# u's spectrum blocks loaded by 128 partitions, and inverse transforms moved between the product loop and the waits behind it

## The chip, the core and the metric

The kernel runs on one core of one Trainium2 chip. The metric is the device time of one execution, in microseconds (us). All arithmetic that matters here is float32 or float32r on TensorE (PE), with VectorE (DVE), ScalarE (ACT) and GpSimd (POOL) around it; SyncE (SP), ScalarE and GpSimd issue the transfers.

## What is computed

The reference takes a sequence u of 2048 steps by 512 channels, and runs two blocks on it, each behind a layer norm with learned shift, scale and gate (`sa, ca, ga, sb, cb, gb`, from `silu(c) @ w_mod`):

```
h = layernorm(u) * (1 + ca) + sa
K[d, l] = Re sum_n C[d, n] * exp(dt[d] * A[d, n] * l) * dt[d] * B[d, n]      l = 0 .. 2047
y = irfft(rfft(h, 4096) * rfft(K, 4096))[:2048] + h * Dskip                  per channel
x = u + ga * y
h = layernorm(x) * (1 + cb) + sb
z = gelu(layernorm(h) @ w1), its four channel quarters shifted by +1, -1, +2, -2 steps
x1 = h + z @ w2
out = x + gb * (x1 + gelu(layernorm(x1) @ w3) @ w4)
```

## The kernel before

The kernel is one hand-ordered program; the order in which its Python functions are called is the order of instructions on every engine. It has four parts.

**Part 1** (`turns`, `products`, `burst`, up to about 213 us) builds the convolution kernel K in `KX`, norms u, and takes the first half of the Fourier transform of u (`u_dft`). Its results go to a DRAM buffer `VU` of [2 channel halves, 64 rows, 64 columns, 256 channels]. The 64 rows are real and imaginary parts of 32 frequencies; which row holds what follows from the columns of the constant `FU`. VU's rows are real parts of frequencies 0 to 31, then the imaginary ones.

**Part 2** is a loop over 16 steps `(jh, kc)`: two channel halves `jh`, eight groups `kc` of four frequencies. Step n does `spectrum_k(n)` (the second half of K's transform, line 667), `multiply(n)` on VectorE (lines 678 to 683), `back(n-1)` (the first half of the inverse transform, line 693; ScalarE evicts `z`, and GpSimd writes it to the DRAM buffer `ZT[jh]`) and `spectrum_u(n+1)` (line 644), which needs u's block. `load_vu` (line 633) brings a block in by two transfers on SP, one for the real parts to partitions 0 to 63 and one for the imaginary parts to partitions 64 to 127, three steps ahead. The last step's two writes of `z` are issued by ScalarE.

Inside the loop's later turns the second half of the inverse transform for the first channel half runs: `load_inv(0, g)` reads two blocks of `ZT[0]`, and `inverse(0, g)` is two calls of `inv_half` (line 722), each of four matmuls into a PSUM tile, and an addition on VectorE (line 725) into `X2`, the residual. There are four groups g of four sequence blocks. Groups 0 to 2 are transformed in turns 11 to 13, group 3 behind the loop. `ldw1` and `ldw2` load w1 and w2 in two parts each; the `split` they return makes a high and a low part on ScalarE and VectorE (line 744).

All of these loads take their buffers in turn from one pool of seven (`ldp`, tile name `ld`), so a load waits for the readers of the buffer seven places earlier.

**The waits.** `ZT[1]` can only be read when its last write has landed. Behind the loop stand `inverse(0, 3)`, ten statistics of first halves (`half_stat`), and filler matmuls, `keep(n)` (line 1140), n products of w1 with itself into a tile that nobody reads. Then come the transforms of the second channel half in the order in which the mixer needs them: group 3's second part (blocks 14 and 15, mixer group 7), then `a00`, `a30`, `a01` (group 0's first part, group 3's first, group 0's second), and `a10`, `a11` (group 1). A name like `a00` stands for the addition of that part on VectorE; its matmuls are issued where `inv_half` is called. SP issues the loads in this order, group 1 and group 2 as whole blocks of 512 KB, the others as 256 KB. A second `keep` stands behind `a01`'s matmuls.

**Part 3 and 4**, the token mixer (`mix_mod1`, `mix_mod2`, `mix_norm`, `transposed`, `parts_of`, `mix_half`, lines 762 to 828) and the channel mixer (`chan`, lines 860 to 961), follow by groups of two blocks. For one mixer group: VectorE modulates and takes statistics (`mix_mod2`, lines 765 and 758), GpSimd makes the reciprocal deviation (lines 753, 754, 814, 815), ScalarE norms, TensorE transposes (line 790), ScalarE and VectorE split the transposes (`nh`, `nl`, line 798), and TensorE does 24 products for each of two halves (lines 825 to 828).

Of the kernel before, what the change touches and what calls it, by code (L numbers as in the profile page):

```python
# [12 lines left out]
PSUM = bass.MemoryType.PSUM  # L13
# [14 lines left out]
def shape_constants():  # L28
    f = lambda x: np.ascontiguousarray(x.astype(np.float32))
    k1, k2, q = np.arange(32), np.arange(64), np.arange(32)  # L30
    c2b = lambda c: np.where(c < 32, 31 - c, c)
    th = 2 * np.pi * (k1[None] + .5) * q[:, None] / 64
    W = np.stack([np.cos(th), -np.sin(th)], 1)
    FU = np.zeros((4, 32, 2, 2, 2, 32))
    for h in range(2):
        for cp2 in range(2):
            cp = 2 * h + cp2
            FU[1 - cp if cp < 2 else cp, :, h, cp2] = W
    FK = np.zeros((2, 2, 32, 2, 64))
    FK[:, 0, :, 0] = FK[:, 1, :, 1] = W.reshape(32, 64)  # L40
    b = c2b(np.arange(64))
    al = 2 * np.pi * b[:, None, None] * ((k1[None, :, None] + .5) / 4096 + k2[None, None, :] / 64)
    c, s = np.cos(al), np.sin(al)
    T2 = np.stack([np.stack([c, -s], 2), np.stack([s, c], 2)]).reshape(128, 32 * 128)
    T3 = np.stack([s, -s]).reshape(128, 32 * 64)
    h, cq, cp2 = np.meshgrid(np.arange(2), np.arange(16), np.arange(2), indexing='ij')
    b = c2b((2 * h + cp2) * 16 + cq).reshape(64)
    al = 2 * np.pi * b[None, :] * k2[:, None] / 64
    c, s = np.cos(al), np.sin(al)
    Gm = np.zeros((64, 2, 64, 2))  # L50
    Gm[:, 0, :, 0], Gm[:, 0, :, 1], Gm[:, 1, :, 0], Gm[:, 1, :, 1] = c, s, -s, c
    Gm = np.tile(Gm.reshape(64, 256), (2, 1))
    FI = np.zeros((2, 2, 32, 16, 2, 2, 32))
    for hh in range(2):
        for c2 in range(2):
            for cc in range(16):
                bb = int(c2b(np.array((2 * hh + c2) * 16 + cc)))
                th = 2 * np.pi * (k1[:, None] + .5) * (bb + 64 * q[None]) / 4096
                FI[c2, 0, :, cc, hh, bb // 16 - 2 * hh] = np.cos(th) * (2 / 4096)
                FI[c2, 1, :, cc, hh, bb // 16 - 2 * hh] = -np.sin(th) * (2 / 4096)  # L60
    eye = np.eye(16)
    j = np.arange(32)
    c0 = np.tile((eye[:, :, None] * (j + .5)).reshape(16, 512), (2, 1))
    C0 = np.zeros((2, 2, 32, 2, 512))
    C0[:, 0, :, 0], C0[:, 1, :, 1] = c0, c0
    C0 = C0.reshape(128, 1024)
    e1 = (eye[:, :, None] * j).reshape(16, 512)
    e2 = (eye[:, :, None] * np.ones(32)).reshape(16, 512)
    C1 = np.concatenate([e1, e1, e2, e2] * 2, 0)
    ex0 = np.concatenate([np.arange(31, -1, -1), np.arange(32, 64)])  # L70
    ex1 = np.concatenate([64 * np.arange(8), 512 * np.arange(4)])
    CE = np.concatenate([(eye[:, :, None] * ex0.reshape(2, 32)[:, None, None, :]).transpose(1, 0, 2, 3).reshape(16, -1),
                         np.zeros((16, 64 * NX1))], 1)
    CE = np.tile(CE, (8, 1))
    for u in range(4):
        CE[u * 32:u * 32 + 32, 1024 + u * 16 * NX1:1024 + (u + 1) * 16 * NX1] = \
            np.tile((eye[:, :, None] * ex1).reshape(16, -1), (2, 1))
    PA = np.zeros((2, 4, 16, 2, 2, 4, 2, 16))
    PB = np.zeros((4, 2, 16, 4, 4, 2, 4, 16))
    for e in range(16):  # L80
        for v in range(2):
            for u in range(4):
                for p in range(2):
                    PA[v, u, e, v, p, u, p, e] = 1
        for c in range(8):
            for p in range(4):
                PB[c // 2, c % 2, e, c // 4 * 2 + c % 2, p, 1 - c // 2 % 2, p, e] = 1
    return {k: f(v) for k, v in dict(
        FU=FU.reshape(128, 256), FK=FK.reshape(128, 128), T2=T2, T3=T3, G=Gm,
        FI=FI.reshape(128, 16 * 128), C0=C0, C1=C1, CE=CE, PA=PA.reshape(128, 512), PB=PB.reshape(128, 2048), ID=np.eye(128)).items()}  # L90
# [16 lines left out]
def dram(t, off, ap):  # L107
    return bass.AP(tensor=t.tensor, offset=t.offset + off, ap=ap)


def body(ctx, tc, A):
    nc = tc.nc
    V, S, P, T, Y = nc.vector, nc.scalar, nc.gpsimd, nc.tensor, nc.sync
# [74 lines left out]
    FU = ph.tile([128, 2, 128], F32, name="FU")  # L188
# [440 lines left out]

    def load_vu(jh, kc):  # L630
        t = vus[jh, kc] = block()
        for ri in range(2):
            Y.dma_start(t[ri * 64:ri * 64 + 64],
                        dram(VU, jh * 1048576 + (ri * 32 + kc * 4) * 16384, [[256, 64], [16384, 4], [1, 256]]))

    def spectrum_u(jh, kc):
        vu = vus.pop((jh, kc))
# [48 lines left out]
    def back(jh, kc):  # L686
        zc = zcs.pop((jh, kc))
        z = s2.tile([128, 4, 256], F32, name="z")
        o = [psa.tile([128, 2, 256], F32, name="pz") for kk in range(2)]
        for n in range(2):  # L690
            for kk in range(2):
                r = slice(kk * 64, kk * 64 + 64)
                T.matmul(o[kk], Gm[r, n], zc[n][r], start=(n == 0), stop=(n == 1))  # L693
        for kk in range(2):
            act(z[:, 2 * kk:2 * kk + 2], o[kk])
            if (jh, kc) == (1, 7):
                S.dma_start(ZT[jh][:, kc * 4 + 2 * kk:kc * 4 + 2 * kk + 2], z[:, 2 * kk:2 * kk + 2])
        if (jh, kc) != (1, 7):
            P.dma_start(ZT[jh][:, kc * 4:kc * 4 + 4], z)

    def load_inv(jh, g, i=None, qs=(Y, Y)):
        if (jh, g) not in zis:
            zis[jh, g] = [block() for h in range(2)]
        for h in range(2):
            c0 = 12 - 4 * g if h == 0 else 4 * g
            a, n = (0, 4) if i is None else (2 * (i if h else 1 - i), 2)
            qs[h].dma_start(zis[jh, g][h][:, a:a + n],  # L707
                            dram(ZT[jh], (h * 16 + c0 + a) * 32768, [[256, 128], [32768, n], [1, 256]]))
# [18 lines left out]
    def inverse(jh, g):  # L727
        for i in range(2):
            inv_half(jh, g, i, psy, "py")()
# [353 lines left out]
    with tc.manual_schedule():  # L1083
# [12 lines left out]
        for n, st in enumerate(steps):  # L1096
            p = spectrum_k(*st)
            multiply(*st, us, p)
            if n == 7:
                v0x.close()  # L1100
                pw2 = ctx.enter_context(pool("pw2", side="right", reuse_waits="tile"))
                pw1 = ctx.enter_context(pool("pw1", side="right", reuse_waits="tile"))
                W2h, W2l, ldw2 = weights(pw2, A["w2"], 512, 512, "w2", 4)
                W1h, W1l, ldw1 = weights(pw1, A["w1"], 512, 512, "w1", 4)
            if n > 0:
                back(*steps[n - 1])
            if n < 15:
                us = spectrum_u(*steps[n + 1])
            if n + 3 < 16:
                load_vu(*steps[n + 3])  # L1110
            if n == 0:
                load_t2(1)
            if n == 1:
                Y.dma_start(T3[:, 16:], t3[:, 16:])
            if n in (3, 4, 6, 8):
                load_x(n - 3 if n < 5 else n // 2 - 1)
            if n == 9:
                Y.dma_start(FI, A["FI"].rearrange("p (a b c) -> p a b c", a=16, b=2))
            if split:
                split()  # L1120
                split = None
            if n in (8, 9, 14, 15):
                split = (ldw1 if n < 10 else ldw2)(two, n % 2 * 2, 2)
            if 9 <= n < 13:
                load_inv(0, n - 9)
            if 11 <= n < 14:
                inverse(0, n - 11)
        back(*steps[15])
        split()
        s2x.close()  # L1130
        tp = lambda name, bufs=1, **k: pool(name, bufs, reuse_waits="tile", **k)
        cm = ctx.enter_context(tp("cm", 2, side="right"))
        hv = ctx.enter_context(tp("hv", side="right"))
        gop = ctx.enter_context(tp("gop", 2, side="right"))
# [8 lines left out]
        load_inv(1, 0, 0, (Y, S))  # L1143
        load_inv(1, 3, 0)
        load_inv(1, 0, 1)
        inverse(0, 3)
        for b in (14, 15, 0, 1, 2, 3, 4, 5, 6, 7):
            half_stat(b, 0)
        load_inv(1, 1)
        keep(14)  # L1150
        inv_half(1, 3, 1, psy, "py")()
        first_stats(7)
        load_inv(1, 2)
        a00 = inv_half(1, 0, 0, psy, "py")
        a30 = inv_half(1, 3, 0, psw, "pm")
        a01 = inv_half(1, 0, 1, psw, "pm")
        keep(22)
        mix_mod1(7)
        a00()
        mix_mod2(7, 0)  # L1160
        mix_mod2(7, 1)
        mix_norm(7)
        first_stats(0)
        a30()
# [2 lines left out]
        hl = parts_of(transposed(mh.pop(7)[0]))  # L1167
        mix_mod2(0, 0)
        mix_mod2(0, 1)
        a10 = inv_half(1, 1, 0, psy, "py")  # L1170
        a11 = inv_half(1, 1, 1, psy, "py")
        mix_half(7, hl, 0)
        mix_norm(0)
        first_stats(1)
# [95 lines left out]
```

## Time and profile before

| | us |
|---|---|
| three runs | 718.76, 717.22, 712.0 |
| median | 717.22 |
| profiled execution | 716.82 |
| its span, first to last instruction | 715.1 |
| TensorE busy | 671.7 |
| VectorE busy | 506.3 |
| ScalarE busy | 335.6 |
| mean granted TensorE clock | 0.993 |

Instructions stand in the profile by engine, line and operation, with the tile written and the tiles read. Matmuls are PE and weight loads PEld. ScalarE's instructions all have line 119, that of a helper. "issue" as what ended an idle time says that the engine waited for nothing that the profile shows. SPq, ACTq and POOLq are the transfers that these engines issue. The granted clock is a share of full speed.

### The profile page before, as it was taken

How to read it: one execution, taken by the hardware profiler on the slowest of the kernel's cores; microseconds unless marked ns; L12 is line 12 of the kernel's file. 1: busy time of each engine (PE TensorE's matmuls, PEld its weight loads, DVE VectorE, ACT ScalarE, POOL GpSimd, SP SyncE). 2: the span in 40 equal slices, each digit the busy share in tenths (PEclk: the TensorE clock that was granted, in tenths of full speed). 3: DMA queues.
4: the chain of work that ended last, by engine and by line, in shares of the span. 5: the costliest groups of instructions: out<-in, count | busy, mean ns of one | idle time of the engine just before them, and what ended most of it. 6: DMA issues, size and time to landing. Idle time of an engine off the chain costs nothing.

```text
span 715.1 us, 16869 instructions
## 1 busy us (share of the span) xinstructions
PE 671.7 (94%) x7083; PEld 520.1 (73%) x7083; DVE 506.3 (71%) x847; ACT 335.6 (47%) x549; POOL 85.6 (12%) x191
## 2 busy tenths in 40 slices
PE   2689999999999899998899999999999999999997
PEld 1356655666568566664688889989898998989896
DVE  8989999999986566767978868557463635454422
ACT  2768898889956255634245623313123121212121
POOL 1011212112000001100463200201010000000000
PEclk9999999999999999999999999999999999999999
DMA  8452274744439999793649402011020111111011
GB/s 286 152 129 69 74 217 102 191 128 116 132 80 266 232 289 315 224 324 144 217 149 302 132 5 56 15 45 31 16 74 16 49 27 31 31 30 30 0 30 31
DMA packets 56884, 85.52 MB, mean 120 GB/s; under 512 B 5764, under 2 KB 43656, under 8 KB 55144
## 3 DMA queue, kind: packets, MB, share of 16 engines
q1 hardware_dynamic: 52648, 66.61, 34.8%
q0 software_dynamic: 3136, 16.52, 6.4%
q10 hardware_dynamic: 1024, 1.31, 0.6%
q8 instruction: 56, 0.92, 0.5%
q14 instruction: 20, 0.16, 0.1%
HBM read 58.20 MB, written 31.85 MB: 126 GB/s over the span
## 4 chain that ended last, share of the span: by engine, by line
PE 48%; DVE 2%; ACT 1%; DMA 1%; SPq 0%; issue 0%; POOL 0%; DVEq 0%; ACTq 0%
PE pm L825 7%; PE pm L828 7%; PE pm L826 7%; PE pa L949 6%; PE pa L941 6%; PE pa L942 5%; PE ph L879 2%; PE ph L880 2%; PE ph L882 2%; PE pT L790 2%; DMA ld<-ZT 1%; PE pT L1140 1%; PE py L722 1%; ACT nh L119 0%; DVE st L758 0%; SPq L707 0%
## 5 line engine op out<-in xcount | busy, mean ns | idle before, releaser
L119 ACT ACTIVATE gh<-pm 128x512 fp32r<-128x512 f32 (+1 forms) x48 | 26.9, 560 | 200.7 <-PE pm L828 200.7
L825 PE MATMUL pm<-nh,w3h 128*128 128x256 f32 (+1 forms) x352 | 85.8, 279 | 0.9 <-ACT nh L119 0.9
L826 PE MATMUL pm<-nh,w3l 128*128 128x256 f32 (+1 forms) x352 | 85.6, 279 | 0.1
L933 DVE TENSOR_TENSOR gl<-gf,gh 128x512 fp32r<-128x512 f32 (+1 forms) x48 | 30.8, 642 | 68.4 <-ACT gf L119 68.4
L941 PE MATMUL pa<-w4h,gh 128*128 128x512 f32 (+1 forms) x176 | 69.6, 396 | 0.0
L942 PE MATMUL pa<-w4l,gh 128*128 128x512 f32 (+1 forms) x176 | 68.9, 392 | 0.0
L825 PEld LDWEIGHTS pm<-nh,w3h 128*128 128x128 f32 (+1 forms) x352 | 65.3, 185 | 2.6 <-ACT nh L119 1.1
L826 PEld LDWEIGHTS pm<-nh,w3l 128*128 128x128 f32 (+1 forms) x352 | 65.2, 185 | 2.2 <-DVE w3l L744 0.5
L828 PE MATMUL pm<-nl,w3h 128*128 128x256 f32 (+1 forms) x352 | 54.8, 277 | 0.0
L949 PE MATMUL pa<-w4h,gl 128*128 128x512 f32 (+1 forms) x176 | 48.1, 391 | 0.8 <-DVE gl L933 0.8
L458 PE MATMUL xx<-MG,ON 64*128 64x512 f32 x160 | 48.0, 396 | 0.0
L457 PE MATMUL xx<-MG,ON 64*128 64x512 f32 x160 | 48.0, 396 | 0.0
L828 PEld LDWEIGHTS pm<-nl,w3h 128*128 128x128 f32 (+1 forms) x352 | 46.7, 185 | 0.2 <-DVE nl L798 0.2
L753 POOL TENSOR_TENSOR rs<-mv,eps_t 128x1 f32<-128x1 f32 (+1 forms) x39 | 11.4, 293 | 279.0 <-DVE mv L759 266.6
L678 DVE TENSOR_TENSOR ma<-pk,us 128x512 f32<-128x512 f32 x32 | 21.9, 685 | 30.7 <-issue 22.9
L119 ACT ACTIVATE z<-pz 128x512 f32<-128x512 f32 x32 | 17.5, 595 | 54.6 <-PE pz L693 38.3
L885 DVE TENSOR_TENSOR h<-h,ph 128x512 f32<-128x512 f32 x16 | 11.0, 686 | 45.2 <-PE ph L882 45.2
L475 DVE SCALAR_TENSOR_TENSOR e<-tr,p 128x512 f32<-128x512 f32 x64 | 41.0, 682 | 2.1 <-ACT tr L119 1.9
L949 PEld LDWEIGHTS pa<-w4h,gl 128*128 128x128 f32 (+1 forms) x176 | 33.0, 188 | 8.3 <-DVE gl L933 1.2
L484 DVE TENSOR_TENSOR e<-tr,p 128x1024 f32<-128x1024 f32 x32 | 38.9, 1217 | 0.0
L507 PEld LDWEIGHTS kp<-e,e 128*32 128x32 f32 x2048 | 30.0, 110 | 12.2 <-issue 8.1
L485 DVE TENSOR_TENSOR e<-tr,m 128x1024 f32<-128x1024 f32 x32 | 38.9, 1216 | 0.0
(234 smaller groups left out, 1763.5 us busy)
## 6 DMA issues: line engine op xcount, KB each, us to landing
VU<-vs SPq DMA_DIRECT2D x64, 128.0 KB, 3.5
ld<-VU SPq DMA_DIRECT2D x32, 256.0 KB, 10.4
ZT<-z POOLq DMA_DIRECT2D x15, 512.0 KB, 8.3
ld<-ZT SPq DMA_DIRECT2D x12, 512.0 KB, 8.2
Dw<-in_w POOLq DMA_DIRECT2D x8, 688.0 KB, 4.7
xu<-in_u SPq DMA_DIRECT2D x16, 256.0 KB, 6.8
KX<-in_u SPq DMA_DIRECT2D x16, 256.0 KB, 10.2
GD<-go SPq DMA_DIRECT2D x16, 256.0 KB, 2.3
```

What stands on the lines that cost most here:

```text
L119: return S.activation(out, in_, f, bias=bias, scale=scale)
L457: T.matmul(x[:, :512], la, ma, start=(i == 0), stop=(i == len(ops) - 1))
L458: T.matmul(x[:, 512:], lb, mb, start=(i == 0), stop=(i == len(ops) - 1))
L475: V.scalar_tensor_tensor(e0[:, 1, a], tr[:, 1, 0], 1.0 - 2.0 * a, mg[:, a], op0=OP.mult, op1=OP.mult)
L484: V.tensor_mul(e0[:, 0], tr[:, 0, 0:1].to_broadcast([128, 2, 512]), mg)
L485: V.tensor_mul(e1.rearrange("p r d q -> p r (d q)"), tr[:, :, 1], m1s[0][:, u % 2:u % 2 + 1].to_broadcast([128, 2, 512]))
L825: T.matmul(p, wh[:, k, c], hi[k], start=(k == 0), stop=False)
L826: T.matmul(p, wl[:, k, c], hi[k], start=False, stop=False)
L828: T.matmul(p, wh[:, k, c], lo[k], start=False, stop=(k == 3))
L941: T.matmul(acc[i], gh[:m, e, s], W4h[:m, f], start=(f == 0), stop=False)
L942: T.matmul(acc[i], gh[:m, e, s], W4l[:m, f], start=False, stop=False)
L949: T.matmul(acc[i], gl[:m, e, s], W4h[:m, f], start=False, stop=(f == 10))
```

## The change

Five things change.

- The columns of `FU` are reordered, so that VU's row 2k is the real and row 2k+1 the imaginary part of frequency k. A block of u then is one access pattern over 128 partitions, and `load_vu` issues one transfer of 512 KB.
- Of the last step's two writes of `z`, SP issues the first and ScalarE the second.
- `inverse(0, 0)` and `inverse(0, 1)` are in turns 11 and 13, `inverse(0, 2)` moves behind the loop, ahead of `inverse(0, 3)`; `load_inv(0, 3)` moves from turn 12 to 13.
- The second part of w2 is loaded behind group 1's blocks of the second half, and split behind `mix_mod2(0, 1)`.
- The matmuls of `a10` and `a11` move from behind the transposes of mixer group 7 to ahead of the second `keep`, with a PSUM pool `psz` of their own; the two `keep` shrink from 14 to 7 and from 22 to 15; and `a00` moves behind `mix_mod2(7, 1)`.

```diff
--- before.py
+++ after.py
@@ -36,6 +36,7 @@
         for cp2 in range(2):
             cp = 2 * h + cp2
             FU[1 - cp if cp < 2 else cp, :, h, cp2] = W
+    FU = FU.reshape(128, 2, 2, 2, 32).transpose(0, 1, 2, 4, 3)
     FK = np.zeros((2, 2, 32, 2, 64))
     FK[:, 0, :, 0] = FK[:, 1, :, 1] = W.reshape(32, 64)
     b = c2b(np.arange(64))
@@ -629,9 +630,7 @@
 
     def load_vu(jh, kc):
         t = vus[jh, kc] = block()
-        for ri in range(2):
-            Y.dma_start(t[ri * 64:ri * 64 + 64],
-                        dram(VU, jh * 1048576 + (ri * 32 + kc * 4) * 16384, [[256, 64], [16384, 4], [1, 256]]))
+        Y.dma_start(t, dram(VU, jh * 1048576 + kc * 8 * 16384, [[256, 128], [32768, 4], [1, 256]]))
 
     def spectrum_u(jh, kc):
         vu = vus.pop((jh, kc))
@@ -694,7 +693,7 @@
         for kk in range(2):
             act(z[:, 2 * kk:2 * kk + 2], o[kk])
             if (jh, kc) == (1, 7):
-                S.dma_start(ZT[jh][:, kc * 4 + 2 * kk:kc * 4 + 2 * kk + 2], z[:, 2 * kk:2 * kk + 2])
+                (Y, S)[kk].dma_start(ZT[jh][:, kc * 4 + 2 * kk:kc * 4 + 2 * kk + 2], z[:, 2 * kk:2 * kk + 2])
         if (jh, kc) != (1, 7):
             P.dma_start(ZT[jh][:, kc * 4:kc * 4 + 4], z)
 
@@ -1119,16 +1118,16 @@
             if split:
                 split()
                 split = None
-            if n in (8, 9, 14, 15):
+            if n in (8, 9, 14):
                 split = (ldw1 if n < 10 else ldw2)(two, n % 2 * 2, 2)
-            if 9 <= n < 13:
-                load_inv(0, n - 9)
-            if 11 <= n < 14:
-                inverse(0, n - 11)
+            if n in (9, 10, 11, 13):
+                load_inv(0, n - 9 if n < 12 else 3)
+            if n in (11, 13):
+                inverse(0, n // 2 - 5)
         back(*steps[15])
-        split()
         s2x.close()
         tp = lambda name, bufs=1, **k: pool(name, bufs, reuse_waits="tile", **k)
+        psz = a2.enter_context(tp("psz", 2, space=PSUM, side="right"))
         cm = ctx.enter_context(tp("cm", 2, side="right"))
         hv = ctx.enter_context(tp("hv", side="right"))
         gop = ctx.enter_context(tp("gop", 2, side="right"))
@@ -1143,22 +1142,26 @@
         load_inv(1, 0, 0, (Y, S))
         load_inv(1, 3, 0)
         load_inv(1, 0, 1)
+        inverse(0, 2)
         inverse(0, 3)
         for b in (14, 15, 0, 1, 2, 3, 4, 5, 6, 7):
             half_stat(b, 0)
         load_inv(1, 1)
-        keep(14)
+        split = ldw2(two, 2, 2)
+        keep(7)
         inv_half(1, 3, 1, psy, "py")()
         first_stats(7)
         load_inv(1, 2)
         a00 = inv_half(1, 0, 0, psy, "py")
         a30 = inv_half(1, 3, 0, psw, "pm")
         a01 = inv_half(1, 0, 1, psw, "pm")
-        keep(22)
+        a10 = inv_half(1, 1, 0, psz, "pz")
+        a11 = inv_half(1, 1, 1, psz, "pz")
+        keep(15)
         mix_mod1(7)
-        a00()
         mix_mod2(7, 0)
         mix_mod2(7, 1)
+        a00()
         mix_norm(7)
         first_stats(0)
         a30()
@@ -1167,8 +1170,7 @@
         hl = parts_of(transposed(mh.pop(7)[0]))
         mix_mod2(0, 0)
         mix_mod2(0, 1)
-        a10 = inv_half(1, 1, 0, psy, "py")
-        a11 = inv_half(1, 1, 1, psy, "py")
+        split()
         mix_half(7, hl, 0)
         mix_norm(0)
         first_stats(1)
```

## The prediction

> **What bounds the kernel now.** I read the page first, then the windows, then the matmul and weight-load timelines of the middle of the run, then the other engines there. Times are microseconds from the start of the span.
>
> ```profile
> span 715.1 us, 16869 instructions
> PE 671.7 (94%) x7083; PEld 520.1 (73%) x7083; DVE 506.3 (71%) x847; ACT 335.6 (47%) x549; POOL 85.6 (12%) x191
> q8 instruction: 56, 0.92, 0.5%
> ld<-VU SPq DMA_DIRECT2D x32, 256.0 KB, 10.4
> ```
>
> TensorE is busy for 94% of the span, so the edits count only where they lengthen or shorten its order of work. They touch two stretches: the loop over the 16 products (about 228 to 333) and the two waits behind it (333 to 371), where the second half's transform results go to DRAM and come back. q8 is the queue that brings instructions: 56 packets of some 16 KB.
>
> The loop, first in the timeline of weight loads (start, length, and in brackets the idle time before and its releaser):
>
> ```profile
> 231.94 0.13 PEld L667 LDWEIGHTS pk<-VK,xu 64*64 64x64 f32 x2 [0.90 <-issue]
> 241.04 0.19 PEld L667 LDWEIGHTS pk<-VK,xu 64*64 64x64 f32 x2 [0.38 <-issue]
> 244.58 0.22 PEld L667 LDWEIGHTS pk<-VK,xu 64*64 64x64 f32 x3 [3.35 <-issue]
> 248.03 0.30 PEld L693 LDWEIGHTS pz<-zc,Gm 64*128 64x128 f32 x4 [0.17 <-issue]
> 251.83 0.21 PEld L667 LDWEIGHTS pk<-VK,xu 64*64 64x64 f32 x8 [0.38 <-issue]
> 253.74 0.30 PEld L693 LDWEIGHTS pz<-zc,Gm 64*128 64x128 f32 x4 [0.17 <-issue]
> ```
>
> The windows (length; busy time of PE, PEld, DVE, ACT, POOL; granted clock, busy share of the transfer engines, GB/s), then the data queue in a view of 230.3 to 241.5 (packets, MB, share), then SP's timeline:
>
> ```profile
> 222.00:224.00 2.00, 2.00 (x41) 2.00 (x40) 1.60 (x3) 1.41 (x3) 0.00 (x0) 1.00 1.16 200
> 244.00:246.00 2.00, 1.51 (x29) 1.42 (x32) 0.00 (x0) 0.00 (x0) 0.00 (x0) 0.59 0.96 228
> 246.00:248.00 2.00, 2.00 (x42) 1.86 (x34) 0.00 (x0) 0.00 (x0) 0.00 (x0) 0.56 1.01 336
> 346.00:348.00 2.00, 2.00 (x12) 1.32 (x8) 1.93 (x5) 0.00 (x0) 0.23 (x1) 1.00 1.10 350
> ```
>
> ```profile
> q1 hardware_dynamic: 1632, 2.46, 109.3%
> ```
>
> ```profile
> 217.04 5.66 SPq L633 DMA_DIRECT2D ld<-VU  x6
> ```
>
> An undisturbed spectrum of K (L667) takes 251.83 to 253.74, 1.91 us from its first weight load to the next line's. The one that begins at 241.04 takes until 248.03, 6.99 us: TensorE stops for 3.35 us "issue" (no semaphore is waited for), and the two windows after it have a granted clock of 0.59 and 0.56, where the others quoted have 1.00. So this stop costs 6.99 - 1.91 = **5.08 us**. In 230.3 to 241.5, the stretch ahead of it, no packet of q8 is listed, while q1, the data, is at 109%: I read the stop as TensorE running out of instructions behind data. That is a reading; the profile names no releaser. Two rows say what filled the queue. From 217.04 SP issued only u's blocks; the transfers are at share 1.16 there and move 200 GB/s. At 346 to 348 the loads of ZT on 128 partitions move 350 GB/s at share 1.10. u's blocks, 64 partitions a load, keep all engines busy at 57% of the rate.
>
> The two waits, in the timelines of TensorE, ScalarE and VectorE, the chain that ended last, and the row of SP's loads of ZT issued from 341 to 344:
>
> ```profile
> 317.91 1.90 PE L722 MATMUL py<-ld,FI 128*64 128x256 f32 x16
> 319.74 0.45 PE L667 MATMUL pk<-VK,xu 64*64 64x128 f32 x8
> ...
> 341.16 1.08 PE L722 MATMUL py<-ld,FI 128*64 128x256 f32 x8 [2.70 <-DMA ld<-ZT]
> 343.56 3.10 PE L722 MATMUL pm<-ld,FI 128*64 128x256 f32 x16
> 346.60 5.28 PE L1140 MATMUL pT<-w1h 128*128 128x512 f32 x22
> 352.02 1.06 PE L790 MATMUL pT<-ident,h 128*128 128x128 f32 x8
> 353.02 1.95 PE L722 MATMUL py<-ld,FI 128*64 128x256 f32 x16
> 354.90 0.39 PE L825 MATMUL pm<-nh,w1h 128*128 128x256 f32 x1
> ...
> 360.70 1.04 PE L790 MATMUL pT<-ident,h 128*128 128x128 f32 x8
> 362.04 0.39 PE L825 MATMUL pm<-nh,w1h 128*128 128x256 f32 x1 [0.30 <-ACT nh L119]
> ```
>
> ```profile
> 333.19 0.60 ACT L119 ACTIVATE z<-pz 128x512 f32<-128x512 f32 x1 [1.66 <-issue]
> 333.82 0.35 ACTq L697 DMA_DIRECT2D ZT<-z  x1
> 334.22 0.60 ACT L119 ACTIVATE z<-pz 128x512 f32<-128x512 f32 x1 [0.43 <-PE py L722]
> 350.66 0.82 ACT L119 ACTIVATE h<-h,nm,rs 128x512 f32<-128x512 f32 x1 [0.38 <-POOL nm L815]
> 358.54 1.51 ACT L119 ACTIVATE h<-h,nm,rs 128x512 f32<-128x512 f32 x2
> ```
>
> ```profile
> 335.89 1.29 DVE L744 TENSOR_TENSOR w2l<-ld,w2h 128x512 fp32r<-128x512 f32 x2 [3.35 <-ACT w2h L119]
> 345.41 0.68 DVE L725 TENSOR_TENSOR KX<-py,KX 128x512 f32<-128x512 f32 x1
> 362.02 1.29 DVE L798 TENSOR_TENSOR nl<-pT,nh 128x512 fp32r<-128x512 f32 x2 [1.16 <-ACT nh L119]
> ```
>
> ```profile
> 334.85 2.02 DMA ZT<-z
> ```
>
> ```profile
> L707 SPq DMA_DIRECT2D ld<-ZT x3: 359/360/442, 341.1 to 342.6; - x3
> DMA to landing us min/median/max: 6.0/6.7/7.5
> ```
>
> The last z is written at 334.85, lands 2.02 later (336.87), and only then the loads of ZT begin. TensorE has 2.70 idle until 341.16 and keeps its clock at that. Then three halves of transforms run to 346.66, 22 filler products (0.24 each) to 351.88, and the transposes of mixer group 7 start at 352.02. The next two halves (L722, 1.95) stand between these transposes and the group's first product, at 354.90.
>
> **The change part by part.**
>
> *u's blocks.* Sixteen loads of 512 KB on 128 partitions take the place of 32 of 256 KB on 64; FU's columns are reordered on the host for it, and no matmul changes. By itself the loop does not wait for these blocks. The price of the new load is not in the trace; the nearest row is ZT's load, the same access pattern on another tensor: 0.52 MB at 350 GB/s is 1.5 us, against 2.6 at 200. Seven blocks are loaded ahead of the stop, so some 7 x 1.1 = 8 us of queue are gone by 241. Bounds of what that does to the stop: nothing (it stays, 5.08) or all of it (it goes). I take all: the packet that was wanted came at the end of a backlog that is 8 us shorter now, and the other stop of the kind, 0.90 at 231.94, is short. **-5.08**, with both ends in the range.
>
> *One transform less in the loop.* inverse(0,2) goes from turn 13 to behind back(15), and turns 12 and 13 share what 11 to 13 did. L722 runs from 317.91 to 319.74 there with TensorE dense on both sides: **-1.83**. SP issues the load of group 3 a turn later, still more than a turn before its use; W2's first half, queued behind it, waits as long and is wanted two turns on.
>
> *First wait.* inverse(0,2) adds 1.9, keep(7) for keep(14) takes 7 x 0.24 = 1.7 away. This is covered by the idle 2.70, of which some 2.1 stays; without that cover it would be +0.2. Of the last two writes the first moves from ACT's queue to SP's. ACT's second z started at 334.22, after the issue at 333.82; it can start when the first z ends, 333.80, so the write and all loads behind it are 0.42 earlier: **-0.42**. On SP the write stands ahead of the ZT loads, which wait for it anyway. The second half of W2 leaves this wait too (VectorE's 1.29 at 335.89); two more additions of 0.68 come in its place, so VectorE is as far as before when the first load lands: 0.
>
> *Second wait.* Here I work in the times of before. Halves a10 and a11 now follow a01 at 346.66, but they need both loads of group 1. The row of loads has issues at 341.1 to 342.6 with landings after 6.0 (347.1, the first) and 7.5 (350.1, the third); the middle one, the second of group 1, is then at 348.6. So TensorE does a quarter of a half at 347.1, stops, and has 1.7 left at 348.6: it ends near 350.4 with the pair, and keep(15) adds 3.6: 354.0. The transposes wait for nothing else: a00 moved behind mod2 makes the norm's end (350.66 + 0.82 = 351.48) 0.6 earlier, since a00's 0.68 at 345.41 leaves that chain. But keep(15) is in order ahead of them. So the transposes are at 354.0, **2.0 late**; the products follow 1.34 after (360.70 to 362.04 shows that distance): 355.35, only 0.45 later than 354.90, as the pair no longer stands between.
>
> What is late next: VectorE splits group 7's transposes before it modulates group 0, so ScalarE's norm of group 0 (end 358.54 + 1.51 = 360.05) is also 2.0 late, 362.05. TensorE's products, 5.8 long, are done at 361.15 and wait. Transposes of group 0: 362.1 for 360.70, 1.4 late. The moved split puts its two VectorE operations, 1.29, behind mod2(0,1). VectorE had 1.16 of slack at 362.02, so it is free at 360.86 + 2.0 + 1.29 = 364.15, while group 0's split is due at 362.02 + 1.4 = 363.4: 0.7 late, of which I give TensorE 0.6. Sum of the second wait: 1.4 + 0.6 = **+2.0**. Its bounds: +0.1 if group 1 has landed by 346.7 (pair and keep(15) then end at 352.1), and +3.0 if ScalarE's part of the split, about as long, lies on the path too. The W2 load of that split follows group 1's in the queue, so by the same rate it lands near 350, some 6 us before ScalarE gets there. From here TensorE is dense to the end.
>
> **The sum.** The profiled execution took 716.82, 1.7 over its span of 715.1 and 0.4 under the median of 717.22. 716.82 - 5.08 - 1.83 - 0.42 + 2.0 = **711.5**. Of the three runs before, one is 712.0 and two are at 717 and 719: a gap of 5 to 7, about one such stop. I count on the median of the changed kernel as a run without it.
>
> **Rivals.**
>
> *The stop stays* (716.6). The queue is as full as before, only with other data: SP runs further ahead and x's loads come earlier. For it: q1 is over 100% busy all through 230 to 241, and freed queue time is refilled. Against it: rates of 350 for 200 shorten any wait behind a fixed number of bytes. 711.5 + 5.08 = 716.6. [...]
>
> *The second wait is free* (709.6). If group 1 lands by 346.7, the term is +0.1 for +2.0. Against it: eight loads of 256 KB are ahead of it in the same queue, which moves a steady 350 GB/s.
>
> *Slower: the stop stays and comes a second time* (721.7). Larger loads let more bytes into the queue ahead of a fetch, and TensorE runs dry twice in the loop, each time with the half clock: 716.6 + 5.08 = 721.7. [...] For it: there is also the stop of 0.90 before 231.94, so one fetch came late before the large one. Against it: the new loads drain faster than they grow.
>
> **How the numbers follow.** Forecast 0.56, stop stays 0.24, second wait free 0.12, slower 0.08. The forecast's own range is 709.5 to 713.5, for the small stops of the loop. All together 708.5 to 718.0. A measurement of this kernel tells about 1% (7.2 us) from no change: faster by that means under 710.05. A fifth of the forecast, two thirds of the free second wait and a share for small stops that go too make 0.26; slower by over 1%, above 724.4, needs a third stop, 0.04; the rest, 0.70, lies within 1%.
>
> **What would show it.** Right: 16 loads of u's blocks of 512 KB; windows at 218 to 228 near 350 GB/s for 200; no window of the loop with a granted clock under 0.9; spectrum to spectrum 5.7 in turn 12; ACT's second z straight behind the first; L722 with an idle time of 1 to 2 ahead of group 1's pair, then fillers, then late transposes; an idle time of about 1 before group 0's transposes, on ACT's norm. Wrong: a stop of over 3 us in the loop, or group 1's pair directly behind a01.

## The result: no change that can be measured

| | before | after |
|---|---|---|
| median of 20 runs each | 717.07 | 716.29 |
| lowest to highest | 712.0 to 720.0 | 713.51 to 720.9 |
| profiled execution | 716.82 | 715.29 |
| its span | 715.1 | 713.5 |

The ratio of the runs is 1.0005, with a 95% interval of 0.9988 to 1.0023: between 0.9 us faster and 1.6 us slower; the 0.8 by which the medians differ lies within that. The forecast, 711.5, was 5.6 under the median of before.

First the page of the changed kernel.

```profile
span 713.5 us, 16809 instructions
PE 671.3 (94%) x7069; PEld 518.0 (73%) x7069; DVE 506.7 (71%) x847; ACT 335.7 (47%) x549; POOL 86.5 (12%) x191
q8 instruction: 56, 0.92, 0.5%
ld<-VU SPq DMA_DIRECT2D x16, 512.0 KB, 15.0
```

TensorE's busy time is within 0.4 of that before, and the 56 instruction packets are the same. The 16 loads of 512 KB are there; from issue to landing one takes 15.0 us, where half as much took 10.4. Windows ahead of the changed loop and in it (the last columns are granted clock, share of the transfer engines and GB/s):

```profile
222.00:224.00 2.00, 2.00 (x41) 2.00 (x40) 1.59 (x3) 1.35 (x3) 0.00 (x0) 1.00 0.93 220
232.00:234.00 2.00, 2.00 (x66) 1.70 (x64) 0.00 (x0) 1.35 (x5) 0.00 (x0) 1.00 1.04 374
244.00:246.00 2.00, 2.00 (x34) 1.14 (x26) 1.20 (x2) 0.00 (x0) 0.00 (x0) 1.00 1.12 213
274.00:276.00 2.00, 1.58 (x9) 0.88 (x11) 1.17 (x2) 0.00 (x0) 0.00 (x0) 1.00 1.04 401
```

The transfers do move faster: of the five windows from 218 to 228, where the forecast had 350, four move 325 to 370, and only the one shown 220. But the engines stay full: at 244 x's loads, 32 partitions each (issued from 236.35 on, landing 10.6 to 13.6 later), move 213 at share 1.12. The weight loads:

```profile
271.54 0.21 PEld L666 LDWEIGHTS pk<-VK,xu 64*64 64x64 f32 x8 [0.39 <-issue]
274.41 0.19 PEld L666 LDWEIGHTS pk<-VK,xu 64*64 64x64 f32 x3 [1.16 <-issue]
```

The stop at 241 is not there. One of the same kind, with no semaphore waited for, is at 274, and it is short, with the clock at 1.00 behind it. Next the second wait, in the timeline of TensorE, with the row of `back(15)` of the kernel before ahead of it:

```profile
331.16 1.99 PE L693 MATMUL pz<-zc,Gm 64*128 64x512 f32 x8 [1.82 <-ACT w2h L119]
```

```profile
327.66 1.99 PE L692 MATMUL pz<-zc,Gm 64*128 64x512 f32 x8 [1.82 <-ACT w2h L120]
336.79 3.08 PE L721 MATMUL py<-ld,FI 128*64 128x256 f32 x16 [1.55 <-DMA ld<-ZT]
339.56 3.33 PE L721 MATMUL pm<-ld,FI 128*64 128x256 f32 x16
343.41 0.62 PE L721 MATMUL pz<-ld,FI 128*64 128x256 f32 x2 [0.53 <-DMA ld<-ZT]
344.81 1.94 PE L721 MATMUL pz<-ld,FI 128*64 128x256 f32 x14 [0.78 <-DMA ld<-ZT]
346.68 3.69 PE L1139 MATMUL pT<-w1h 128*128 128x512 f32 x15
350.53 1.06 PE L789 MATMUL pT<-ident,h 128*128 128x128 f32 x8
359.49 0.98 PE L789 MATMUL pT<-ident,h 128*128 128x128 f32 x7 [1.32 <-ACT h L120]
```

Group 1's pair (`pz`) waits 0.53 and 0.78 for its loads, the 15 fillers follow, and group 7's transposes start 350.53 - 327.66 = 22.87 behind `back(15)`; before it was 352.02 - 331.16 = 20.86. That is 2.0 late, as forecast, and by the way forecast: the pair ends 19.1 behind `back(15)` (346.75), where 19.2 was expected (350.4 in the times of before). The later idle time of 1.32 on ScalarE's norm is the expected one too.

In these two profiled executions the loop, from the first `spectrum_u` to `back(15)`, is 6.05 shorter (103.29 and 97.24), all behind it 1.9 longer, and the loop begins 2.55 later: 1.6 less in all. Part 1, ahead of the loop, does the same work in both.

### The profile page after: what moved, and what is told of

It reads as the page before. It is cut to its first block, busy times and chain, and to the rows that moved or that the text cites. A ratio compares the mean times of both kernels' runs of the same rounds, so it can differ in the third digit from the quotient of the medians.

```text
span 713.5 us, 16809 instructions
## 1 busy us (share of the span) xinstructions
PE 671.3 (94%) x7069; PEld 518.0 (73%) x7069; DVE 506.7 (71%) x847; ACT 335.7 (47%) x549; POOL 86.5 (12%) x191
## 4 chain that ended last, share of the span: by engine, by line
PE 47%; DVE 3%; DMA 2%; ACT 1%; issue 1%; POOL 0%; ACTq 0%; DVEq 0%; SPq 0%
PE pm L824 7%; PE pm L825 7%; PE pm L827 7%; PE pa L948 6%; PE pa L940 6%; PE pa L941 6%; PE ph L879 2%; PE ph L881 2%; PE ph L878 2%; PE pT L789 2%; DMA ld<-ZT 2%; DVE st L757 1%; PE pT L1139 1%; ACT nh L120 0%; DVE h L764 0%
## 5 line engine op out<-in xcount | busy, mean ns | idle before, releaser
L458 PE MATMUL xx<-MG,ON 64*128 64x512 f32 x160 | 49.5, 407 | 0.0
L459 PE MATMUL xx<-MG,ON 64*128 64x512 f32 x160 | 49.5, 407 | 0.0
```

The lines of the kernel that those rows point to most:

```text
L458: T.matmul(x[:, :512], la, ma, start=(i == 0), stop=(i == len(ops) - 1))
L459: T.matmul(x[:, 512:], lb, mb, start=(i == 0), stop=(i == len(ops) - 1))
```

## The experiments

Two theories stood at the start. By one, the stop of 5.08 belongs to the one profiled execution more than to the kernel. By the rival, it is a steady cost that the new loads take away, and something else gives it back. Where an expectation gives the loop's length as 91.8 or 93.4, it runs to `back(14)`, 3.81 before `back(15)`. The "three inverses" in the expectation of rest_alone are one, inverse(0, 2).

Each ratio is to the kernel before in the same series. A difference of two ratios carries the intervals of both, some 2 to 3 us either way; of the single steps below only those from the changed kernel to fill1 and to wait2_undone are clear of zero.

**Before, unchanged.**

> The kernel before, unchanged, profiled a second time. Theory (the 5 us stop at 241 us, priced in the forecast, belongs to the one execution that was profiled): the loop over u's blocks shows no stop of 3 us here, its first spectrum_u to back(15) takes about 98 to 99 us instead of 103.3, and the ratio to the kernel before is 1.000 within 0.002. Rival (the stop is a steady cost that the change takes away and that is lost again elsewhere): a stop of 3 us or more stands in the loop again, with a window of clock near 0.5 behind it, and the loop takes 102 to 104 us.

717.46 (12 runs), ratio 1.001 (0.9984 to 1.0036). What TensorE waited for in the loop, first in the profile shown ahead of the prediction, then in this one (us in total, times, longest):

```profile
PE pk L667 <- issue: 3.8, 2, 3.1
```

```profile
PE pk L667 <- issue: 0.8, 1, 0.8
```

The same kernel, with a stop of 0.8 at 248.5. The loop takes 98.96, 4.3 less. Neither the place nor the length of the stop is fixed: 3.1 at 241 in the one execution, 0.8 at 248.5 in the other.

**The loads alone.** `before.py` with the first two edits of the diff.

> The kernel before with only u's blocks read by 128-partition loads; order of the rest untouched. Theory (stop of one execution): the loop's loads land sooner, but no wait of TensorE ended on them, so the time is that of the kernel before, 716 to 717.5. Rival (steady stop, lost again elsewhere): 5 us less in the loop; 711 to 713 if what was lost lies in the rearrangement, 716 to 717 with part 1 about 2.5 us later if the loads themselves move it.

715.9, ratio 0.9992 (0.9970 to 1.0015): at most 2.2 faster. The forecast's 5.08 is outside.

**The rest alone.**

```diff
-    FU = FU.reshape(128, 2, 2, 2, 32).transpose(0, 1, 2, 4, 3)
...
-        Y.dma_start(t, dram(VU, jh * 1048576 + kc * 8 * 16384, [[256, 128], [32768, 4], [1, 256]]))
+        for ri in range(2):
+            Y.dma_start(t[ri * 64:ri * 64 + 64], ...)
```

> The changed kernel with u's blocks read by two 64-partition loads each as before: only the rearrangement (inverse(0, 2) behind the loop, the second write of z by the other queue, group 1's products in the second wait). Theory: the rearrangement's own terms are all there is, -1.83 (three inverses' 24 matmuls and additions out of the loop) -0.15 +2.0 to 2.2 = about 0; 716 to 717.5, the loop about 1.8 us shorter than that of the unchanged kernel on the same chip and the transposes of mixer group 7 about 2.0 later behind back(15). Rival (the stop is steady and the loads remove it): a stop of 3 us stands in this loop too.

718.28, ratio 1.0026 (0.9999 to 1.0052). The stop is back in this profile, in the waits and then in the windows:

```profile
PE pk L667 <- issue: 2.6, 1, 2.6
```

```profile
244.00:246.00 2.00, 2.00 (x52) 1.67 (x44) 0.00 (x0) 0.00 (x0) 0.00 (x0) 0.66 0.99 379
246.00:248.00 2.00, 2.00 (x8) 0.97 (x8) 1.90 (x4) 0.00 (x0) 0.00 (x0) 0.50 1.08 311
```

It is 2.6 long and has the half clock behind it, 4.7 in all; the expectation had no stop here. Against the changed kernel (1.0026 against 1.0005) the old loads cost 1.5, with some 2.3 either way.

**Fewer fillers.** `keep(15)` becomes `keep(1)`.

> The changed kernel with 1 filler matmul in place of 15 behind group 1's products in the second wait. Theory (the fillers end 3.5 us behind ScalarE's norm of group 7, and that is what the wait costs): the transposes of mixer group 7 start about 3.3 us sooner behind back(15), at 19.6 instead of 22.9, and 2.5 to 3.3 of it reaches the end: 713 to 714. Rival (what follows is bound by VectorE, not by the fillers): the products wait longer for group 0's norm instead, and the time stays within 1 of the changed kernel's. A second rival: without fillers TensorE idles at once into a window of half clock, 1.7 us lost, 715.

713.03, ratio 0.9961 (0.9934 to 0.9988), 3.2 less than the changed kernel by the ratios. TensorE:

```profile
344.02 0.49 PE L1139 MATMUL pT<-w1h 128*128 128x512 f32 x1
344.66 1.06 PE L789 MATMUL pT<-ident,h 128*128 128x128 f32 x8
354.01 0.98 PE L789 MATMUL pT<-ident,h 128*128 128x128 f32 x7 [1.32 <-ACT h L120]
```

Group 7's transposes are 19.88 behind `back(15)` (324.78 here) for 22.87, and no half clock followed, which had cost 5.08 - 3.35 = 1.73 behind the long stop of the kernel before: the eight transposes take 1.06, as they do in the changed kernel at a clock of 1.00, and the mean clock of this execution is 0.999. ScalarE's norm, which they need, ends in the changed kernel at 347.02, by its timeline of ScalarE, while the fillers run to 350.4:

```profile
346.21 0.81 ACT L120 ACTIVATE h<-h,nm,rs 128x512 f32<-128x512 f32 x1 [0.38 <-POOL nm L814]
```

**The second wait undone.** `a10` and `a11` back behind the transposes, `keep(22)`, `a00` and the split of w2 at their old places.

> The changed kernel with the whole of the second wait as before: group 1's products behind the transposes of mixer group 7, 22 fillers, a00 and the second split of W2 at their old places. Left of the change: u's loads, inverse(0, 2) behind the loop, the second z write. Theory (the second wait costs what was forecast, +2.0 to 2.2 at group 0's transposes): 2 less than the changed kernel's 716.5, so 714 to 715, group 0's transposes 2 sooner behind back(15). Rival (the second wait is free, and what the rearrangement costs comes from elsewhere, the transform behind the loop): no gain, 716 to 717.

714.29, ratio 0.9972 (0.9948 to 0.9997): 2.4 less than the changed kernel by the ratios, 2.0 by the medians. Group 0's transposes are 30.0 behind `back(15)`, for 31.8 in the changed kernel. The timeline of TensorE shows what the split of w2 does at its old place:

```profile
328.89 1.99 PE L692 MATMUL pz<-zc,Gm 64*128 64x512 f32 x8 [1.82 <-ACT w2h L120]
335.06 1.95 PE L721 MATMUL py<-ld,FI 128*64 128x256 f32 x16 [2.31 <-DVE KX L724]
349.39 0.30 PE L789 MATMUL pT<-ident,h 128*128 128x128 f32 x1
350.32 0.99 PE L789 MATMUL pT<-ident,h 128*128 128x128 f32 x7 [0.63 <-ACT h L120]
```

With the split here, `inverse(0, 3)` waits 2.31 for VectorE to add `inverse(0, 2)`, and of group 7's transposes the first is 20.5 and the other seven are 21.4 behind `back(15)`. So with the split at its old place the transform behind the loop brings a wait of its own; what that costs at the end was not measured apart.

**No data for u.** fill1 without the loads of u's data from the fourth block on; it leaves out 6.8 MB that the result needs, and is a time without them, not a version. In `load_vu`:

```diff
+        if (jh, kc) not in steps[:3]:
+            P.memset(t, 0.0)
+            return
```

> fill1 (1 filler), but from the fourth of u's 16 blocks on a block is filled with zeros by GpSimd instead of read from DRAM: 13 loads of 512 KB, 6.8 MB, leave the loop's queue. Leaves out the loading of the data, so this is a time without that traffic and not a version. Theory (TensorE's stop in the loop is an instruction packet that comes late behind data): no stop over 0.5 anywhere in the loop, first spectrum_u to back(15) 91.8 instead of 93.4; about 1.7 less than fill1, 711 to 712. Rival (the stop is not the data's doing, such as a fixed place in the code or a wait of the sequencer): a stop of 1.2 to 1.7 stays and the time is fill1's, 713.

710.29, ratio 0.9923 (0.9896 to 0.9950), 2.7 less than fill1, with as much uncertainty. From the third turn on every turn without a transform takes 5.70, with one 7.43; TensorE's waits in the loop hold no "issue" line at all, the longest is

```profile
PE pk L669 <- DVE mb L681: 0.5, 1, 0.5
```

The queues from 2.0 to 17.5 after the first `spectrum_u`, for fill1 (whose stop of 1.4 comes 19.3 after it), then without u's data:

```profile
q1 hardware_dynamic: 2107, 3.85, 106.8%
q8 instruction: 1, 0.02, 0.5%
```

```profile
q1 hardware_dynamic: 595, 3.21, 91.8%
q8 instruction: 2, 0.03, 1.1%
```

With u's data one instruction packet comes in this stretch, without it two, and the stop is gone. The second packet of fill1 comes just behind the stretch, at 245.5, and 2.7 later its stop ends. The other profiles show the same when the queues are read in windows of 0.1 to 0.25 us: all 18 stops of over 0.3 us in the loops of the 13 profiles with u's data end 2.4 to 3.1 us behind a packet of q8. For the long stop of the kernel before, the row that ends it and the window of 241.50 to 241.75:

```profile
244.49 0.61 PE L667 MATMUL pk<-VK,xu 64*64 64x128 f32 x4 [3.12 <-issue]
```

```profile
q8 instruction: 1, 0.02, 37.3%
```

TensorE also runs dry at the same places (the end of a stop less its length): 12.6 behind the first `spectrum_u` in rest_alone and split_old_loads, 19.3 in before_again, fill1 and ahead2, 42.8 in vu_alone, fill1_split and split_again. What differs is when the packet comes. So by these times the stop is a late instruction packet; the profile names no releaser. That data make it late rests on this pair of profiles: the second packet behind the first `spectrum_u` comes 18.0 after it with u's data and 13.6 without, the fourth 34.3 and 26.1. The transfer engines are 92% busy even without u's data, with 595 packets for 2107; whether bytes, packets or something else decides is not shown.

Of the 150 packets in these 13 loops, of some 16 KB each (0.92 MB in 56), 18 came so late that TensorE stopped for over 0.3 us.

**The split of w2 later.** fill1 with

```diff
         mix_mod2(0, 1)
-        split()
...
         mix_half(0, hl, 0)
+        split()
```

> fill1 with the second split of W2 moved further back, from behind mix_mod2(0, 1) to behind the first half of mixer group 0, beyond VectorE's and ScalarE's work for the transposes of groups 0. Theory (the split's 1.27 on VectorE and 1.16 on ScalarE stand in the chain to group 0's transposes, which idle 1.32 on ScalarE's norm): the idle before those transposes falls from 1.3 to under 0.3 and 0.6 to 1.1 of it reaches the end: 712 to 713 against fill1's 713.3. Rival (VectorE is the bound of these turns and the split only moves to another one of them): the same time as fill1 within 0.4, with a new idle before the transposes of group 1.

711.52, ratio 0.9936 (0.9908 to 0.9964), 1.8 less than fill1 by the ratios. Group 0's transposes:

```profile
355.61 0.99 PE L789 MATMUL pT<-ident,h 128*128 128x128 f32 x7 [0.49 <-ACT h L120]
```

The idle time is 0.49 for 1.32, where under 0.3 was expected. As a second series this kernel gave 712.45:

> fill1_split, unchanged, a second time, as the base of the runs beside it. Theory: 711 to 712, the loop with one stop of 1.6 to 2.5 near 272 or 247, no idle over 0.3 before group 0's transposes. Rival (its 711.5 was a lucky draw of the half-clock windows of the first 100 us): 713.

Its ratio is 0.9942 (0.9915 to 0.9969), and its loop has one stop of 0.6, less than expected. It is the version that beats both kernels: the one before by 4.2 to 4.6 us, which is under 1%.

**The old loads in that version.**

> fill1_split with u's blocks read by two 64-partition loads each, as in the kernel before: the loads alone, in a kernel that is otherwise the fastest so far. Theory (either form leaves a stop in the loop, 1.65 to 5.1 long in the three profiles with the old loads, 1.6 to 4.2 in the seven with the new ones, and the mean differs by 1 to 2): 0.8 to 2 more than fill1_split, 712.5 to 713.5, and a stop between 1.6 and 5.1 in the profile. Rival (the forecast: the new loads take 5.08 away): 5 more, 716.5.

714.83, ratio 0.9981 (0.9948 to 1.0014): the loads are worth 2.8 here by the ratios, with intervals that allow 0 to 6. Three comparisons of the loads alone, 0.6, 1.5 and 2.8, average 1.6.

**Two trials to shorten the stop.** x's loads later, and u's blocks two steps ahead in place of three:

```diff
-            if n in (3, 4, 6, 8):
-                load_x(n - 3 if n < 5 else n // 2 - 1)
+            if n in (6, 7, 8, 10):
+                load_x(n - 6 if n < 9 else 3)
```

> fill1_split with the 16 loads of x moved from turns 3, 4, 6, 8 to turns 6, 7, 8, 10, out of the stretch in which u's blocks and T's second half fill the queue. Nothing is left out. Theory (the loop's remaining stop of 1.65 is the queue's doing): no stop, or one under 0.8, between 240 and 280; 1 to 1.6 less than fill1_split, about 711. Rival (the queue is full for as long, only later): a stop of 1.5 comes later in the loop, the time stays. Slower rival: u's blocks are late behind x and TensorE waits on a load of u in turns 8 to 11, 2 or more.

```diff
-            if n + 3 < 16:
-                load_vu(*steps[n + 3])
+            if n + 2 < 16 and n > 0:
+                load_vu(*steps[n + 2])
```

> fill1_split with u's blocks loaded two turns ahead in place of three, from turn 1 on: the same bytes, 512 KB less of them in the queue at a time. Theory (an instruction packet waits behind what is queued on its transfer engine, so a shorter queue shortens the stop): the stop falls from 1.65 to under 1, 0.5 to 1.5 less, 710 to 711. Rival (the queue is full whatever is ahead): same stop, 711.4. Slower rival: TensorE waits on u's loads, seen as idle ended by DMA ld<-VU in turns 3 to 8, 2 to 5 more.

x_later: 710.35, ratio 0.9922 (0.9893 to 0.9952); a stop stays (1.3), and whether the kernel is faster than fill1_split can't be told. ahead2: 712.45, ratio 0.9943; in its waits

```profile
PE pk L666 <- issue: 3.9, 2, 2.8
```

512 KB less in the queue did not shorten the stops, and the ratio is that of fill1_split. This expectation fell. (The profiled executions of x_later, ahead2 and inverse1_out lie 4.8, 3.4 and 3.9 above the medians of their runs, so their stops need not be typical.)

**One more transform out of the loop.** `inverse(0, 1)` ahead of `inverse(0, 2)`, one filler left of seven.

> fill1_split with inverse(0, 1) also out of the loop and behind back(15), where it takes the place of 6 of the 7 fillers of the first wait. Theory (TensorE has room in the first wait for work that is of use, and what is short there is VectorE): the loop is 1.73 shorter, TensorE's idle of 1.6 to 1.9 ahead of the first landing load falls to 1.3, VectorE's two more additions of 0.69 leave 0.5 of their 1.38 behind its idle of 0.86; net -1.2: 710.2. Rival (VectorE's chain to mixer group 7 takes all of it): group 7's transposes 1.4 or more later behind back(15) and nothing won, 711.4.

712.06, ratio 0.9942 (0.9912 to 0.9971): nothing measured. The loop is 1.73 shorter in its turns, group 0's transposes are 1.0 later behind `back(15)`; the 0.7 that remains is below what the runs resolve. Its profile has the longest stop of all:

```profile
PE pk L666 <- issue: 4.2, 2, 3.8
```

Up to turn 13 this loop is that of split_again, and both were profiled on the same chip: stops of 3.8 and of 0.6 come out of the same instructions.

## Why the prediction was wrong

The loop from the first `spectrum_u` to `back(15)`, in the timelines of all 14 profiles. Without stops it takes 95.6 (no_u_loads), 97.3 with the third transform in it (7.43 - 5.70 more), 93.9 in inverse1_out; "stops" is what lies over that, half clock included.

| kernel | u's loads | first spectrum_u at | loop | stops |
|---|---|---|---|---|
| before | 64 partitions | 227.87 | 103.29 | 6.0 |
| before_again | 64 | 229.21 | 98.96 | 1.6 |
| rest_alone | 64 | 228.13 | 100.25 | 4.7 |
| split_old_loads | 64 | 228.85 | 101.42 | 5.8 |
| after | 128 | 230.42 | 97.24 | 1.7 |
| vu_alone | 128 | 229.77 | 98.92 | 1.6 |
| fill1 | 128 | 227.51 | 97.27 | 1.7 |
| wait2_undone | 128 | 229.16 | 99.73 | 4.1 |
| fill1_split | 128 | 229.50 | 97.99 | 2.4 |
| split_again | 128 | 230.57 | 96.66 | 1.1 |
| x_later | 128 | 231.84 | 97.45 | 1.9 |
| ahead2 | 128 | 229.19 | 101.86 | 6.3 |
| inverse1_out | 128 | 228.75 | 101.20 | 7.3 |
| no_u_loads | none | 228.69 | 95.59 | 0 |

- **u's blocks, -5.08: the step that failed.** The sum took the stop of one execution as what every execution pays, and let all of it go. With the old loads it is 1.6 to 6.0 (mean 4.5 of four), with the new ones 1.1 to 7.3 where the loop is that of before or after, at least up to turn 13 (mean 2.8 of seven). The ranges overlap, so that it is shorter is not shown by the profiles; it moves to another packet, and it does not go. In the runs the loads alone are worth 0.6 to 2.8, each with an interval that reaches zero. The argument "seven blocks, 8 us less of queue ahead of the packet" held for one packet only. The first that comes more than 2 us behind the first `spectrum_u` comes 9.0 to 13.6 behind it with the old loads and 6.2 to 9.0 with the new, and in none of the nine profiles with the new loads is there a stop at its place. But 11 to 13 packets come in a loop, and later ones were late in all nine. There 512 KB less ahead (ahead2) shortened nothing, only taking the data away did.
- **The check that misled.** The profiled execution was near the median, so its stop looked typical. But its part 1 ended at 227.87, the second earliest of 14 between 227.51 and 231.84, and that hid a loop among the slowest. The 712.0 among three runs was read as a run without the stop; the unchanged kernel's second profile took 713.47 with a stop of 1.6 still in it.
- **inverse(0,2), -1.83:** right, near enough; the turn falls from 7.43 to 5.70, by 1.73.
- **The last write, -0.42:** a third of it. The second z follows the first at once, but the write then takes longer:

```profile
330.81 2.41 DMA ZT<-z
```

  It lands 5.56 behind `back(15)` for 5.71, 0.15 less: the write takes 2.41 where it took 2.02.
- **Second wait, +2.0:** right in place and size, 2.0 at group 7's transposes, 2.3 at most of group 0's (31.8 behind `back(15)` for 29.5), 2.0 to 2.4 in the runs with it undone. Its bulk is the fillers that stand in order behind a late load (3.2 with fill1); moving the split on was worth 1.4 to 1.8, not clear of zero, for 0.6 in the sum.
- **The rivals.** "The stop stays", 716.6, is what came nearest, though in a shorter form. ahead2 agrees with it: 512 KB less of backlog did not help, its longest stop is 2.8. But a fetch is not free of data either: the second packet comes 4.4 later in fill1 than in no_u_loads (18.0 and 13.6), and with the new loads the first one comes sooner (6.2 to 9.0 for 9.0 to 13.6). "The second wait is free" fell: it cost its 2.0. Two stops in a loop, as the slower rival had it, came in three profiles with the new loads (wait2_undone, ahead2, inverse1_out), but not in that of the changed kernel. The half clock that this rival counts with each stop stands behind 2.6 in rest_alone (0.66 and 0.50), but not behind the one of the changed kernel (1.16 in the weight loads, 1.00).

The term of the loads at 1.6 in place of 5.08 and the write at 0.15 make the sum -1.6 - 1.83 - 0.15 + 2.0 = -1.6 against a measured ratio of 1.0005 (0.9988 to 1.0023, at most -0.9). With that mean at least 0.7 is unexplained; with the 0.6 of vu_alone the sum is -0.6, which the interval allows. rest_alone points to a remainder too: its ratio of 1.0026 is 1.9 where the terms without the loads make 0; the interval reaches to 0, so this stays open.

## What to carry to other kernels

A stop that waits for no semaphore can be a draw, not a constant (3.1 and 0.8 in two executions of the kernel before): look in the queues for an instruction packet just ahead of its end, profile the same kernel again before a forecast takes the stop away, and ask what becomes of the next packets. Compare stretch by stretch, since an execution near the median can be an early first part and a late second. Fillers meant to keep TensorE's clock are work in order: put none of them between a late load and what comes next (with 1 for 15 the mean clock was 0.999 here). When work moves into a wait, price the engine that takes over its result too; here, with the split left in the first wait, TensorE waited 2.31 for VectorE.

## What the runs showed of the hardware

The half clock came behind idle times as short as 2.49, and not behind all that were longer. Behind 2.70 idle in the first wait of the kernel before the clock stayed at 1.00 (340 to 346); in the second profile of the same kernel the idle time there was 2.49, and the windows behind it, in that profile, show it halved:

```profile
337.92 3.48 PE L722 MATMUL py<-ld,FI 128*64 128x256 f32 x16 [2.49 <-DMA ld<-ZT]
```

```profile
336.00:338.00 2.00, 0.09 (x2) 0.12 (x4) 2.00 (x7) 0.00 (x0) 0.00 (x0) 1.00 1.03 362
338.00:340.00 2.00, 1.93 (x12) 0.92 (x14) 1.40 (x4) 0.00 (x0) 0.00 (x0) 0.63 1.09 353
340.00:342.00 2.00, 2.00 (x14) 1.26 (x12) 1.90 (x7) 0.00 (x0) 1.03 (x3) 0.52 1.10 350
```

Behind the stops of 2.6 (rest_alone), 2.8 (ahead2), 3.12 (before) and 3.8 (inverse1_out) the lowest window has 0.50, 0.50, 0.56 and 0.50. Behind 2.31 (wait2_undone) sixteen matmuls of line 721 took 1.95, where the sixteen behind the 2.49 above took 3.48. From the first `spectrum_u` to 346 us, idle times of up to 2.31 kept the clock in all 14 profiles; of the eight from 2.49 to 3.83 only the one of 2.70 did. So the length of the idle time alone does not decide; what does is not shown.
